# First pair of batches: one product M per batch, two pairs of heads side by side, in a new order of steps

## Chip, core, metric

The kernel runs on one core of one Trainium2 chip. The time is that of one execution in device microseconds; lower is better. In the texts PE or TensorE is the matmul engine (PEld its weight loads), DVE or VectorE, ACT or ScalarE, POOL or GpSimd the others, SP the engine that issues most DMAs. Times inside the execution count from the start of its span.

## The reference

Two attentions by way of 32 packed rows, then two feed-forward blocks; weights come as 64-bit floats and are converted on the chip.

```python
p_packed = sm_attn(p, k, v)              # 8 batches, 8 heads, 576 tokens, 64 dims, 32 packed rows
out = sm_attn(q, p_packed, p_packed)
x = out.transpose(0, 2, 1, 3).reshape(4608, 512)
a = x @ w1                               # 512 x 1024
b = x @ w2
x = ((a * b) @ w3) @ w_out               # 1024 x 1024, 1024 x 512
h = x @ w_in                             # 512 x 2048
return np.maximum(0.01 * h, h) @ w_out2  # 2048 x 512
```

## The kernel before

The eight batches are done as four pairs. For one batch, `a` and `b` are not made from the attention's output: the 32 packed rows of each head (ppM) are first multiplied with w1 and w2, which gives M, and the attention weights of the second softmax (AT, 4 heads x 32 rows = 128 partitions, in two units g of four heads) are then multiplied with M. Products that must be exact to nearly 32 bits are made of three passes over a number's high and low part (`three`); the parts come from a split: ScalarE casts the value to the high part, VectorE or GpSimd subtracts it.

The first pair (batches 0 and 1) has the weights' conversion beside it, and its order is written out by hand: `SCRIPT` is a list of steps, played one after the other. Each engine takes its instructions in a fixed order; a scheduler makes this order from the steps, and may move an instruction past some of another step. The steps that matter here, with unit u = 0, 1 for batch 0 and 2, 3 for batch 1:

- k, q, v, p: loads. s, e, n, t, y: scores, exponential, norm, transposition and values of the first attention, up to ppM. S, E, N, x: the same for the second, up to AT (x: ScalarE's cast and GpSimd's subtraction, L263 and L108).
- l, c, d with a key (w: w1 and w2 together, 16 pieces; o: w_out, 8; 3: w3, 16) and a number: load of a piece (L296, tile c64 with three buffers, 0.524 MB), conversion (ScalarE L278, VectorE L280 and L284), and GpSimd's addition (L287), for w with a store of the converted piece, which later pairs read back (L312).
- M, a, b: product M of a feature block fc (L406) and its splits for the first and the second batch (L425, L108). U packs the ppM of both batches in one tile pp32P of 128 columns. Z closes one set of PSUM pools and opens the next.
- A with fc, batch n, token half th: `ab_unit`, 12 matmuls of 288 columns for `a` and as many for `b` come as one step of 12 in the trace (L105, mm<-AT,M); ScalarE copies `a` (L460), VectorE multiplies (L462, here "product"), and the result is stored in DRAM. A step uses two of four PSUM tiles mm, so a step waits for the product of the step two before it.
- o, O, h, H: splits of w_out and of w3. W with fc and half: product of w3 and w_out (L105, mm<-ab,wsp), which makes the matrix W13; it needs mm tiles too.

Behind the script follow the x2 stage of the pair (mm<-ab,W), the other three pairs in loops, and the second feed-forward block.

Of the kernel before, what the change touches and what calls it, by code (L numbers as in the profile page):

```python
# [7 lines left out]

SCRIPT = """k2 k0 p0 s0 lw0 p1 k1 v0 cw0 lw1 k3 q0 e0 v2 s1 v1 s2 e1 n1 cw1 t0 lo0 n0 t1 lw2 dw0 e2 dw1 y0 S0 cw2 q1 v3 E0 s3 y1 n2 S1 q2 lw3 E1 lo1 t2 y2 lo2 e3 N0 co0 N1 x0 t3 S2 q3 x1 n3 E2 cw3 y3 U dw3 M0 N2 lw4 x2 co1 S3 dw2 Z cw4 lo3 dw4 a0 lw5 E3 lw6 N3 M1 x3 A000 b0 a1 A001 co3 do0 lw7 cw5 cw6 A011 do1 do3 A010 lo4 co2 dw5 do2 lw8 cw7 b1 A101 O1 dw6 A110 cw8 M2 lw11 dw8 co4 O0 A100 lw9 a2 dw7 cw9 lw10 A200 M3 A201 lo5 b2 O2 p2 a3 lw12 A210 dw9 A111 do4 cw10 p3 A211 lo6 A300 M4 b3 lw13 cw11 O3 A301 co5 A310 dw10 co6 o4 dw11 do5 a4 lo7 cw12 do6 b4 l30 A400 lw14 k4 lw15 A410 o5 o6 l31 A311 A411 dw12 M5 A401 co7 cw13 a5 l35 dw13 A501 do7 cw14 b5 c30 M6 cw15 A511 A510 o7 l33 a6 dw15 c31 b6 c35 d31 l37 A601 c33 dw14 d30 A600 l32 k6 M7 A611 H0 a7 k5 c37 b7 A610 c32 l34 A700 d33 d35 H3 d32 A701 d37 c34 h1 l38 d34 l315 H2 H5 H4 A711 h7 s4 c38 d38 W00 l36 c36 l39 l310 d36 h6 c39 l311 H8 e4 l312 W01 t4 A500 W10 W20 s5 c311 A710 v4 k7 d39 l313 d311 c310 c312 e5 c313 d310 h9 W30 v5 d312 H11 W21 h10 s6 l314 W11 n4 c314 d313 d314 q4 v7 W31 y4 t5 W40 s7 H12 q5 W41 h13 W50 n5 e6 v6 c315 d315 n6 H14 t6 W51 y5 e7 H15 y6 W60 n7 W61 W70 W71"""
KQ = {"k": 1}
F32 = mybir.dt.float32
F32R = mybir.dt.float32r
# [6 lines left out]
P = 128  # L21
# [11 lines left out]
def tile_kernel(ctx, tc, qT, kT, vL, pT, w12, w3b, wo1, win, wo2, out):  # L33
# [23 lines left out]
    def ps_m():  # L57
        return ps_pv() if psum["early"] else ps_tile([P, 512], "m", 2)
# [48 lines left out]
    def sub(engine, out, x, hi):  # L107
        engine.tensor_tensor(out=out, in0=x, in1=rd(hi), op=ALU.subtract)  # L108
# [79 lines left out]

    def att_t(b, g):
        pt = Ps.pop((b, g))  # L190
        if b < 2 and not psum["early"]:
            ps, tail = ps_m(), ps_m()
        else:
            t = ps_t()
            ps, tail = t[:, 0], t[:, 1]
        for c in range(4):
            nc.tensor.transpose(ps[:, c * P:(c + 1) * P], pt[:, c:512:4], ident)
        nc.tensor.transpose(tail[:64, :P], pt[:, 512:576], ident)
        PT = att.tile([P, 5, P], F32, tag="PT", name="PT", bufs=2)
        nc.scalar.copy(PT[:, 0:4].rearrange("p c s -> p (c s)"), ps)  # L200
        nc.scalar.copy(PT[:64, 4], tail[:64, :P])
        PTs[b, g] = PT

    def att_pv(b, g):


        PT = PTs.pop((b, g))
        _, st = s1p.pop((b, g))
        ps = ps_m() if b < 2 else ps_pv()
        v = [vs.pop((b, g, j)) for j in range(2)]  # L210
        for c in range(5):
            K = P if c < 4 else 64
            for j in range(2):
                r = slice(j * 64, j * 64 + 64)
                nc.tensor.matmul(ps[r, :P], PT[:K, c, r], v[j][:K, c, :], start=c == 0, stop=c == 4)  # L215
        pp = att.tile([P, P], F32, tag="pp", name="pp", bufs=1)
        nc.scalar.mul(pp, ps[:, :P], st[:, 3:4])
        nc.tensor.transpose(ps[:, 2 * P:3 * P], pp, ident)
        pv = ps[:, 2 * P:3 * P].rearrange("p (j c) -> p j c", j=2)
        for h in range(2):  # L220
            r = slice(h * 64, h * 64 + 64)
            nc.scalar.copy(ppM[b % 2][r, 2 * g:2 * g + 2, h * 32:h * 32 + 32], pv[r, :, h * 32:h * 32 + 32])

    def pair_up(p):

        for i in range(2):
            for j in range(2):
                c = (j ^ i) * 64
                x = ppM[i][:, j::2]
                if whole(2 * p):  # L230
                    nc.scalar.copy(pp32["P"][:, j::2, c:c + 64], x)
                else:
                    hi, lo = (ppP[:, a, j::2, c:c + 64] for a in range(2))
                    nc.scalar.copy(hi, x)
                    sub(nc.vector, lo, x, hi)

    def s2_mm(b, g):
        ps = scores(ppM[b % 2], "q", b, g, b % 2)
        t = att.tile([P, 18, 32], F32, tag="sT", name="sT", bufs=2)
        nc.vector.transpose(out=t.rearrange("p (a n) c -> p a (n c)", a=2), in_=ps[:, :, :TH])  # L240
        st = att.tile([P, 18, 2], F32, tag="st2", name="st2", bufs=2)
        nc.vector.tensor_reduce(out=st[:, :, 0:1], in_=t, axis=AX.X, op=ALU.max)
        nc.vector.tensor_tensor(out=t, in0=t, in1=st[:, :, 0:1].to_broadcast([P, 18, 32]), op=ALU.subtract)
        s2p[b, g] = t, st
# [318 lines left out]
    def attention_b(p):  # L563

        d = {s: [] for s in range(16)}
        for s, x in attention_a(p).items():
            if s >= 16:
                d[s - 16] += x
        us = units(p)
        for u, (b, g) in enumerate(us):  # L570
            s = (1, 4, 7, 10)[u]
            d[s] += [lambda b=b, g=g: s2_mm(b, g)]
            if u < 2:
                d[s + 1] += [lambda x=us[u + 2]: load_kq("q", *x)]
# [150 lines left out]
    def w13_step(fc, h):  # L725
# [11 lines left out]
        "d": lambda k, i: conv_end(k, i),  # L737
        "o": lambda i: split_wo1(i, nc.vector), "O": lambda i: split_wo1(i, nc.gpsimd),
        "h": lambda i: split_half("3", i, nc.gpsimd), "H": lambda i: split_half("3", i, nc.vector),
        "U": pack, "Z": late, "M": lambda i: m_mm(0, i), "a": lambda i: m_split(0, i, 0), "b": lambda i: m_split(0, i, 1),  # L740
        "A": ab_step, "W": w13_step,
        "r": lambda fc, th: reload_ab(0, fc, th), "f": lambda fc, th: split_ab(abr.pop((0, fc, th)), fc, th),
    }
    for x in SCRIPT.split():
        if x[0] in "lcd":
            steps[x[0]](x[1], int(x[2:]))
        elif x[0] in "AWrf":
            steps[x[0]](*(int(y) for y in x[1:]))
        else:
            steps[x[0]](*([int(x[1:])] if x[1:] else []))  # L750
# [293 lines left out]
```

## Time and profile before

| what | value |
|---|---|
| time, median of 3 runs | 1363.05 us (1358.98 to 1367.06) |
| the profiled execution: time / span | 1364.38 us / 1362.6 us |
| mean granted clock of TensorE | 0.988 |
| TensorE busy | 1315.1 us, 97% of the span |
| VectorE, ScalarE, GpSimd busy | 948.8, 701.1, 184.1 us |
| DMA | 323.48 MB, mean 237 GB/s |

The span runs from the first to the last instruction of the profiled execution; the 1.8 us between span and time lie around it. Busy times are sums over the engine's instructions; where instructions overlap a little or wait for a shared resource while they run, that is in them. The DMA share is the mean busy share of the core's 16 DMA engines.

### The profile page before, as it was taken

The numbers are of one execution on the slowest core, as the hardware profiler recorded it, in microseconds if no ns is written. First come the engines' busy times: TensorE is split into PE (matmuls) and PEld (weight loads), VectorE is DVE, ScalarE is ACT, GpSimd is POOL, SyncE is SP. The second block draws the span as 40 slices with busy tenths as digits, with TensorE's granted clock in tenths as the row PEclk, the third lists the DMA queues.
The fourth block names the chain that finished last, engine by engine and source line by source line (L and its number), as shares of the span: only waits on it lengthen the run. The fifth ranks groups of instructions, "written<-read, shape, count | busy, mean of one in ns | idle before, by whom it ended". The sixth has DMA issues, their size and how long they took to land.

```text
span 1362.6 us, 23490 instructions
## 1 busy us (share of the span) xinstructions
PE 1315.1 (97%) x8512; PEld 1255.7 (92%) x8512; DVE 948.8 (70%) x1588; ACT 701.1 (51%) x1365; POOL 184.1 (14%) x148
## 2 busy tenths in 40 slices
PE   6799999999999999999999999999999999999998
PEld 3578999989999999999999999999999999899997
DVE  4899668775987587762977665747665459486657
ACT  4566444675467556753755555545434434344332
POOL 1544521432133312200000000000000000000000
PEclk9799999999999999999999999999999999999999
DMA  9798658767985784397878976467545754878874
GB/s 306 250 304 283 224 158 253 234 200 223 302 280 185 256 271 139 98 307 246 307 262 280 328 260 227 166 209 252 177 152 208 250 187 151 285 260 307 292 265 151
DMA packets 174835, 323.48 MB, mean 237 GB/s; under 512 B 22656, under 2 KB 93312, under 8 KB 174720
## 3 DMA queue, kind: packets, MB, share of 16 engines
q1 hardware_dynamic: 153984, 300.74, 66.0%
q10 hardware_dynamic: 20736, 21.24, 4.5%
q8 instruction: 67, 1.10, 0.3%
q14 instruction: 48, 0.39, 0.1%
HBM read 226.75 MB, written 95.16 MB: 236 GB/s over the span
## 4 chain that ended last, share of the span: by engine, by line
PE 81%; DMA 8%; DVE 3%; issue 1%; ACT 1%; SPq 0%; ACTq 0%; DVEq 0%
PE mm L105 29%; PE b L899 26%; PE c L899 13%; PE a L899 7%; DMA xh<-xfd 4%; PE m L105 3%; PE at L163 2%; DMA c<-w3b 1%; PE at L215 1%; DVE cT L284 1%; DMA wi<-wid 1%; DVE cT L280 1%; DMA xl<-xfd 1%; DMA v<-vL 0%; DMA c<-w 0%
## 5 line engine op out<-in xcount | busy, mean ns | idle before, releaser
L105 PE MATMUL mm<-AT,M 128*128 128x288 f32 x1536 | 232.0, 302 | 13.9 <-DVE ab L462 4.1
L105 PEld LDWEIGHTS mm<-AT,M 128*128 128x128 f32 x1536 | 211.3, 190 | 27.4 <-ACT a L460 6.5
L899 PE MATMUL b<-xh,wi 128*128 128x384 f32 x768 | 218.7, 337 | 6.9 <-DMA xh<-xfd 5.6
L899 PE MATMUL b<-gh,wo 128*128 128x384 f32 x768 | 214.0, 336 | 1.4 <-DVE o L862 1.4
L105 PEld LDWEIGHTS mm<-ab,W 128*128 128x128 f32 x1536 | 204.4, 188 | 6.1 <-issue 5.5
L105 PE MATMUL mm<-ab,W 128*128 128x288 f32 x1536 | 209.9, 296 | 0.0
L899 PEld LDWEIGHTS b<-xh,wi 128*128 128x128 f32 x768 | 140.9, 188 | 9.6 <-DMA xh<-xfd 3.9
L899 PEld LDWEIGHTS b<-gh,wo 128*128 128x128 f32 x768 | 140.7, 188 | 2.0 <-issue 1.0
L899 PE MATMUL b<-xl,wi 128*128 128x384 f32 x384 | 128.9, 336 | 0.0
L899 PE MATMUL b<-gl,wo 128*128 128x384 f32 x384 | 128.6, 335 | 0.0
L667 ACT CAST gh<-gr 128x1152 fp32r<-128x1152 f32 (+1 forms) x72 | 75.6, 1052 | 68.9 <-PE b L899 32.2
L899 PE MATMUL c<-xh,wi 128*128 128x384 f32 x384 | 106.6, 337 | 2.9 <-DMA xh<-xfd 2.9
L899 PE MATMUL c<-gh,wo 128*128 128x384 f32 x384 | 107.3, 336 | 0.2
L108 DVE TENSOR_TENSOR gl<-gr,gh 128x1152 fp32r<-128x1152 f32 (+1 forms) x72 | 87.4, 1218 | 22.7 <-ACT gh L667 22.6
L287 POOL TENSOR_TENSOR c<-cT,c 128x512 int32<-128x512 int32 x56 | 77.7, 1390 | 166.7 <-DVE cT L284 68.7
L108 DVE TENSOR_TENSOR M<-m,M 64x512 fp32r<-64x512 f32 x124 | 84.3, 686 | 20.6 <-ACT M L425 18.1
L667 ACT CAST gh<-gs 128x1152 fp32r<-128x1152 f32 (+1 forms) x54 | 57.0, 1055 | 62.4 <-PE b L899 33.5
L108 DVE TENSOR_TENSOR ab<-ab,ab 128x288 fp32r<-128x288 f32 x128 | 66.5, 545 | 30.7 <-ACT ab L441 30.1
L108 POOL TENSOR_TENSOR wsp<-wsp 128x512 fp32r<-128x512 f32 x48 | 62.6, 1312 | 152.3 <-ACT wsp L385 121.2
L847 ACT ACTIVATE gr<-gr 128x1152 f32<-128x1152 f32 (+1 forms) x54 | 57.3, 1061 | 47.3 <-DVE gr L862 47.0
L425 ACT CAST M<-m 64x512 fp32r<-64x512 f32 x124 | 71.1, 580 | 17.3 <-PE m L105 5.5
L859 ACT COPY gr<-b 128x384 f32<-128x384 f32 x96 | 45.8, 478 | 56.5 <-PE b L899 55.0
(144 smaller groups left out, 2393.6 us busy)
## 6 DMA issues: line engine op xcount, KB each, us to landing
xh<-xfd SPq DMA_DIRECT2D x126, 384.0 KB, 5.4
xl<-xfd SPq DMA_DIRECT2D x126, 384.0 KB, 5.0
part<-o SPq DMA_DIRECT2D x48, 384.0 KB, 3.1
o<-part SPq DMA_DIRECT2D x48, 384.0 KB, 4.2
c<-wo SPq DMA_DIRECT2D x24, 512.0 KB, 5.0
wsp<-w12d SPq DMA_DIRECT2D x48, 256.0 KB, 3.1
abd<-ab ACTq DMA_DIRECT2D x80, 144.0 KB, 3.5
ab<-abd SPq DMA_DIRECT2D x80, 144.0 KB, 3.7
```

The costliest lines, as they stand in the source:

```text
L105: nc.tensor.matmul(dst, lhs(i), rhs(j), start=first and n == 0, stop=last and n == 2)
L108: engine.tensor_tensor(out=out, in0=x, in1=rd(hi), op=ALU.subtract)
L163: nc.tensor.matmul(ps[r:r + 64, th, :TH], w[:, 2 * g + j, :], x[:, th * TH:th * TH + TH], start=True, stop=True)
L215: nc.tensor.matmul(ps[r, :P], PT[:K, c, r], v[j][:K, c, :], start=c == 0, stop=c == 4)
L280: nc.vector.tensor_scalar(out=t, in0=hw, scalar1=3, scalar2=0x3FFFFFFF, op0=ALU.logical_shift_left, op1=ALU.bitwise_and)
L284: nc.vector.scalar_tensor_tensor(out=t, in0=hw, scalar=0xC0000000, in1=t, op0=ALU.bitwise_and, op1=ALU.bitwise_or)
L287: return lambda: nc.gpsimd.tensor_tensor(out=q, in0=t.bitcast(I32), in1=q, op=ALU.add)
L425: nc.scalar.copy(m[r, 0], ps[h ^ n][r])
L667: nc.scalar.copy(hi[step], x[step])
L847: nc.scalar.activation(out=out, in_=x, func=AF.Prelu, alpha=0.01)
L859: nc.scalar.copy(out, ps)
L899: nc.tensor.matmul(dst, lhs(l), rhs(r), start=first and n == 0, stop=last and n == total - 1, skip_group_check=True)
```

## The change

U and pp32P go: M is made for each batch from its own ppM. A matmul then has 64 columns of weights (two heads of 32 rows) instead of 128, and two of them, for j = 0 and 1, write the upper and the lower 64 partitions of one PSUM tile, so that the M of one batch stands in a tile of 128 partitions. Its split is then one cast and one subtraction of 128x512, where there were two and two of 64x512. The converted piece of w is held for two visits (`Wf`). Batch 1 of the first pair no longer has the heads of a pair swapped in its second scores. The other pairs keep their way, with both batches in one product.

```diff
-SCRIPT = """k2 k0 p0 s0 lw0 p1 k1 v0 cw0 lw1 k3 q0 e0 v2 s1 v1 s2 e1 n1 cw1 t0 lo0 n0 t1
...
+SCRIPT = """k0 p0 k1 lw0 v0 s0 v1 cw0 e0 q0 n0 s1 q1 t0 e1 lw1 n1 y0 t1 p1 k2 dw0 S0 y1 cw1
...
-        if b < 2 and not psum["early"]:
-            ps, tail = ps_m(), ps_m()
-        else:
-            t = ps_t()
-            ps, tail = t[:, 0], t[:, 1]
+        t = ps_t()
+        ps, tail = t[:, 0], t[:, 1]
...
-        ps = ps_m() if b < 2 else ps_pv()
+        ps = ps_pv()
...
-        ps = scores(ppM[b % 2], "q", b, g, b % 2)
+        ps = scores(ppM[b % 2], "q", b, g, 0 if alone(b) else b % 2)
...
-            if whole(2 * p):
-                w = converted("w", 2 * fc + g)
-                for j in range(2):
-                    nc.tensor.matmul(
-                        ps[j][:, g * 256:(g + 1) * 256], pp32["P"][:, 2 * g + j], w[:, j * 256:(j + 1) * 256],
-                        start=True, stop=True,
-                    )
-                continue
...
+    def m_alone(b, fc):
+        if fc not in Wf:
+            Wf[fc] = [converted("w", 2 * fc + g) for g in range(2)]
+        ps = ps_m()
+        for g, w in enumerate(Wf.pop(fc) if b else Wf[fc]):
+            for j in range(2):
+                tc.keep_in_program_order(
+                    nc.tensor.matmul(
+                        ps[j * 64:j * 64 + 64, g * 256:(g + 1) * 256], ppM[b][:, 2 * g + j],
+                        w[:, j * 256:(j + 1) * 256], start=True, stop=True,
+                    )
+                )
+        m_ps[b, fc] = ps
+
+    def split_alone(b, fc):
+        ps = m_ps.pop((b, fc))
+        m = main.tile([P, 2, 512], F32R, tag="M", name="M", bufs=3)
+        nc.scalar.copy(m[:, 0], ps)
+        sub(nc.vector, m[:, 1], ps, m[:, 0])
+        Mt[b, fc] = m
```

M and a now take a batch and a block (M03, a03), b is gone. The steps of batch 0 up to its first A steps come first, those of batch 1 behind them; the blocks' M run one A pair ahead; the loads of w_out and w3 come behind those of w; and the A steps A500 and A710, which stood between W steps, stand ahead of W00. From W00 on the script is otherwise as before. Where the order moves the instructions that the numbers below speak of:

TensorE around the first A step (mm<-AT,M). Before:

```order
L163 MATMUL at<-raw,ppM_76 64x288 x4
L218 MATMUL pv<-ident,pp 128x128
L406 MATMUL pv<-w_122,pp32P 128x256 x4
L163 MATMUL at<-raw,ppM_76 64x288 x4
L406 MATMUL m<-w_231,pp32P 128x256 x4
L105 MATMUL mm<-AT,M 128x288 x24
```

Now (ppM_75 is batch 0's, ppM_76 batch 1's; an A step is 12 matmuls):

```order
L425 MATMUL pv<-w_122,ppM_75 64x256 x4
L211 MATMUL pv<-v,PT 64x128 x10
L214 MATMUL pv<-ident,pp 128x128
L105 MATMUL mm<-AT,M 128x288 x12
L162 MATMUL at<-raw,ppM_76 64x288 x4
L105 MATMUL mm<-AT,M 128x288 x12
L425 MATMUL m<-w_294,ppM_75 64x256 x4
L162 MATMUL at<-raw,ppM_76 64x288 x4
L425 MATMUL m<-w_458,ppM_75 64x256 x4
L105 MATMUL mm<-AT,M 128x288 x48
L425 MATMUL m<-w_122,ppM_76 64x256 x4
L162 MATMUL at<-raw,ppad_73 64x288 x4
```

The second scores of batch 1 (at<-raw,ppM_76), which stood ahead of all A steps, now stand among those of batch 0; six A steps lie ahead of batch 1's first M (w_122 with ppM_76), and the seventh, A010, is the next mm<-AT,M behind the last row.

VectorE around the last transposition of batch 1's second softmax, from which its second AT is made. Before, with the first product (L462) behind it:

```order
L108 TENSOR_TENSOR M<-m,M 64x512
L280 TENSOR_SCALAR cT<-c_440 128x512
L255 TENSOR_TENSOR sT<-sT,st_426 128x576
L284 SCALAR_TENSOR_TENSOR cT<-c_440,cT 128x512
L257 STREAM_TRANSPOSE a_458<-sT 128x576
L462 TENSOR_TENSOR ab_485<-mm,a 128x288
```

Now:

```order
L170 TENSOR_REDUCE st<-at 128x1
L277 SCALAR_TENSOR_TENSOR cT<-c_666,cT 128x512
L248 TENSOR_TENSOR sT<-sT,st_499 128x576
L171 TENSOR_SCALAR st<-st 128x1
L273 TENSOR_SCALAR cT<-c_701 128x512
L250 STREAM_TRANSPOSE a_552<-sT 128x576
L277 SCALAR_TENSOR_TENSOR cT<-c_701,cT 128x512
```

Here a_552 stands behind six products and the conversion of the tenth piece of w (c_666) and with the eleventh (c_701), where a_458 stood ahead of the first product and behind the fifth piece of w.

VectorE at the last products ahead of W00. Before (ab_1422 is the 30th product; c_1337 is the seventh piece of w3):

```order
L462 TENSOR_TENSOR ab_1355<-mm,a 128x288
L280 TENSOR_SCALAR cT<-c_1337 128x512
L462 TENSOR_TENSOR ab_1380<-mm,a 128x288
L284 SCALAR_TENSOR_TENSOR cT<-c_1337,cT 128x512
L108 TENSOR_TENSOR ppP<-ppM_75,ppP 128x2x64 x2
L462 TENSOR_TENSOR ab_1422<-mm,a 128x288
```

Now (ab_1366 is the 31st product; c_1508 the eleventh piece of w3 in the order of SP's loads):

```order
L470 TENSOR_TENSOR ab_1314<-mm,a 128x288
L108 TENSOR_TENSOR M<-m,M 128x512
L108 TENSOR_TENSOR wsp<-c_1404,wsp 128x512
L273 TENSOR_SCALAR cT<-c_1508 128x512
L277 SCALAR_TENSOR_TENSOR cT<-c_1508,cT 128x512
L470 TENSOR_TENSOR ab_1366<-mm,a 128x288
L470 TENSOR_TENSOR ab_1396<-mm,a 128x288
```

All 32 products now stand ahead of W00's results, and more conversions of w3 ahead of the last of them.

## Rows read from the trace of the kernel before

**Rows 1.** Busy us of each engine, clock, DMA share and GB/s by stretch

```profile
0.00:37.00 37.00, 24.49 (x159) 14.00 (x159) 16.50 (x35) 14.09 (x35) 8.39 (x15) 0.89 0.90 297
37.00:60.00 23.00, 14.41 (x65) 9.53 (x63) 22.10 (x35) 13.48 (x28) 11.61 (x10) 0.80 0.69 245
60.00:135.00 75.00, 68.61 (x461) 61.37 (x461) 68.68 (x126) 50.02 (x111) 35.32 (x29) 0.96 0.92 295
135.00:160.00 25.00, 23.29 (x186) 22.10 (x187) 18.02 (x30) 11.92 (x25) 15.20 (x11) 0.97 0.64 205
160.00:189.40 29.40, 29.40 (x244) 29.40 (x244) 13.93 (x25) 10.83 (x26) 9.80 (x7) 0.97 0.44 135
```

**Rows 2.** Timeline of TensorE: start us, us, instructions, idle time before

```profile
135.01 1.92 PE L105 MATMUL mm<-ab,wsp 128*128 128x256 f32 x14 [1.61 <-DVE ab L462]
...
141.57 1.74 PE L105 MATMUL mm<-AT,M 128*128 128x288 f32 x12
...
189.39 3.08 PE L105 MATMUL mm<-ab,W 128*128 128x288 f32 x22
```

**Rows 3.** SP's waits to 135 us: total, times, longest

```profile
SPq L296 <- DVE cT L284: 43.5, 20, 8.2
```

**Rows 4.** Groups of VectorE, 60 to 138 us: count, busy us, mean ns

```profile
L284 DVE SCALAR_TENSOR_TENSOR cT<-c,cT 128x512 uint32<-128x512 uint32 x23 | 20.9, 917 | 0.1
L108 DVE TENSOR_TENSOR M<-m,M 64x512 fp32r<-64x512 f32 x26 | 17.8, 685 | 0.7 <-ACT M L425 0.2
L280 DVE TENSOR_SCALAR cT<-c 128x512 uint32<-128x512 uint32 x23 | 14.0, 628 | 3.4 <-POOL ab L108 1.8 <-DMA c<-w 0.8 <-DMA c<-w3b 0.5
L462 DVE TENSOR_TENSOR ab<-mm,a 128x288 f32<-128x288 f32 x30 | 13.3, 449 | 1.6 <-PE mm L105 0.8 <-ACT a L460 0.4
L108 DVE TENSOR_TENSOR wsp<-c,wsp 128x512 fp32r<-128x512 f32 x3 | 3.9, 1288 | 0.0
```

**Rows 5.** Groups of ScalarE, 0 to 190 us

```profile
L425 ACT CAST M<-m 64x512 fp32r<-64x512 f32 x28 | 16.1, 580 | 4.3 <-PE m L406 1.5 <-DVE M L108 1.4 <-PE mm L105 1.0
...
L200 ACT COPY PT<-t 128x512 f32<-128x512 f32 x4 | 2.3, 582 | 2.4 <-PE t L198 2.4
```

**Rows 6.** Timeline of TensorE's matmuls, 102.99 to 111.06 us

```profile
102.99 1.02 PE L406 MATMUL m<-w,pp32P 128*128 128x256 f32 x4
103.67 1.15 PE L105 MATMUL mm<-AT,M 128*128 128x288 f32 x6
104.75 1.19 PE L163 MATMUL at<-raw,ppad 128*64 128x288 f32 x8
105.87 5.32 PE L105 MATMUL mm<-AT,M 128*128 128x288 f32 x38
111.06 1.10 PE L406 MATMUL m<-w,pp32P 128*128 128x256 f32 x4
```

**Rows 7.** Groups of VectorE, 0 to 60 us, second softmax: longest, shortest operation

```profile
L255 DVE TENSOR_TENSOR sT<-sT,st 128x576 f32<-128x576 f32 x4 | 3.7, 925 | 0.1
...
L254 DVE RECIPROCAL st<-st 128x18 f32<-128x18 f32 x4 | 1.0, 244 | 0.0
```

**Rows 8.** Timeline of VectorE: first product, and 30th ahead of W00

```profile
60.10 0.82 DVE L462 TENSOR_TENSOR ab<-mm,a 128x288 f32<-128x288 f32 x2
...
137.47 0.44 DVE L462 TENSOR_TENSOR ab<-mm,a 128x288 f32<-128x288 f32 x1
```

**Rows 9.** DMA from 0 to 135 us: packets, bytes, mean rate

```profile
DMA packets 21910, 38.75 MB, mean 287 GB/s; under 512 B 5454, under 2 KB 9998, under 8 KB 21899
```

**Rows 10.** Two shorter stretches, columns as in rows 1

```profile
50.00:60.00 10.00, 5.74 (x38) 4.55 (x38) 9.90 (x16) 5.96 (x11) 5.29 (x4) 0.97 0.29 97
...
80.00:135.00 55.00, 50.75 (x359) 45.16 (x357) 50.69 (x97) 37.90 (x85) 22.38 (x18) 1.00 0.93 302
```

**Rows 11.** Group of GpSimd, 0 to 138 us: subtraction of AT's split

```profile
L108 POOL TENSOR_TENSOR AT<-a,AT 128x576 fp32r<-128x576 f32 x4 | 6.9, 1735 | 6.0 <-ACT AT L263 5.8
```

**Rows 12.** Timeline of weight loads of the scores in rows 6

```profile
104.74 0.68 PEld L163 LDWEIGHTS at<-raw,ppad 128*64 128x64 f32 x8 [0.16 <-issue]
```

More of the change, by code (lines that the diff above doesn't have):

```diff
@@ L7 @@
 from concourse.masks import make_identity
-SCRIPT = """k2 k0 p0 s0 lw0 p1 k1 v0 cw0 lw1 k3 q0 e0 v2 s1 v1 s2 e1 n1 cw1 t0 lo0 n0 t1 lw2 dw0 e2 dw1 y0 S0 cw2 q1 v3 E0 s3 y1 n2 S1 q2 lw3 E1 lo1 t2 y2 lo2 e3 N0 co0 N1 x0 t3 S2 q3 x1 n3 E2 cw3 y3 U dw3 M0 N2 lw4 x2 co1 S3 dw2 Z cw4 lo3 dw4 a0 lw5 E3 lw6 N3 M1 x3 A000 b0 a1 A001 co3 do0 lw7 cw5 cw6 A011 do1 do3 A010 lo4 co2 dw5 do2 lw8 cw7 b1 A101 O1 dw6 A110 cw8 M2 lw11 dw8 co4 O0 A100 lw9 a2 dw7 cw9 lw10 A200 M3 A201 lo5 b2 O2 p2 a3 lw12 A210 dw9 A111 do4 cw10 p3 A211 lo6 A300 M4 b3 lw13 cw11 O3 A301 co5 A310 dw10 co6 o4 dw11 do5 a4 lo7 cw12 do6 b4 l30 A400 lw14 k4 lw15 A410 o5 o6 l31 A311 A411 dw12 M5 A401 co7 cw13 a5 l35 dw13 A501 do7 cw14 b5 c30 M6 cw15 A511 A510 o7 l33 a6 dw15 c31 b6 c35 d31 l37 A601 c33 dw14 d30 A600 l32 k6 M7 A611 H0 a7 k5 c37 b7 A610 c32 l34 A700 d33 d35 H3 d32 A701 d37 c34 h1 l38 d34 l315 H2 H5 H4 A711 h7 s4 c38 d38 W00 l36 c36 l39 l310 d36 h6 c39 l311 H8 e4 l312 W01 t4 A500 W10 W20 s5 c311 A710 v4 k7 d39 l313 d311 c310 c312 e5 c313 d310 h9 W30 v5 d312 H11 W21 h10 s6 l314 W11 n4 c314 d313 d314 q4 v7 W31 y4 t5 W40 s7 H12 q5 W41 h13 W50 n5 e6 v6 c315 d315 n6 H14 t6 W51 y5 e7 H15 y6 W60 n7 W61 W70 W71"""
+SCRIPT = """k0 p0 k1 lw0 v0 s0 v1 cw0 e0 q0 n0 s1 q1 t0 e1 lw1 n1 y0 t1 p1 k2 dw0 S0 y1 cw1 k3 lw2 E0 S1 s2 v2 dw1 N0 E1 e2 v3 lw3 x0 N1 n2 s3 cw2 t2 x1 e3 dw2 n3 y2 M00 t3 lw4 q2 a00 y3 cw3 Z A000 S2 dw3 A001 lw5 M01 a01 E2 A100 cw4 q3 N2 A101 S3 dw4 lw6 cw5 x2 dw5 M02 a02 E3 A200 cw6 N3 lw7 A201 dw6 cw7 x3 lw8 M10 a10 dw7 A010 A011 M03 a03 cw8 A300 lw9 A301 dw8 cw9 M11 a11 lw10 dw9 A110 A111 M04 a04 cw10 A400 lw11 A401 dw10 cw11 M12 a12 lw12 dw11 A210 lo0 A211 M05 a05 cw12 A500 lw13 A501 dw12 co0 cw13 M13 a13 lw14 dw13 do0 A310 A311 lo1 M06 a06 cw14 A600 O0 lw15 A601 co1 dw14 cw15 lo2 do1 M14 a14 dw15 co2 O1 A410 lo3 do2 A411 M07 a07 co3 lo4 O2 A700 do3 co4 lo5 A701 M15 a15 O3 do4 l30 A510 co5 lo6 do5 o4 A511 c30 co6 l31 M16 a16 o5 p2 A610 d30 lo7 do6 c31 A611 o6 l33 M17 a17 co7 d31 H0 l35 do7 c33 A710 h1 p3 o7 A711 k4 d33 c35 l32 H3 d35 l37 c32 H5 d32 l34 c37 H2 k5 d37 c34 l38 k6 l315 d34 H4 h7 s4 c38 d38 W00 l36 c36 l39 l310 d36 h6 c39 l311 H8 e4 l312 W01 t4 W10 W20 s5 c311 v4 k7 d39 l313 d311 c310 c312 e5 c313 d310 h9 W30 v5 d312 H11 W21 h10 s6 l314 W11 n4 c314 d313 d314 q4 v7 W31 y4 t5 W40 s7 H12 q5 W41 h13 W50 n5 e6 v6 c315 d315 n6 H14 t6 W51 y5 e7 H15 y6 W60 n7 W61 W70 W71"""
@@ L148, in load_p, with alone @@
             nc.sync.dma_start(out=ppad[b % 2][r, :, h * 32:h * 32 + 32], in_=pT[r, b])
-    pp32 = {}
-    def whole(b):
+    def alone(b):
         return b < 2
@@ L222, in att_pv, with pair_up @@
             nc.scalar.copy(ppM[b % 2][r, 2 * g:2 * g + 2, h * 32:h * 32 + 32], pv[r, :, h * 32:h * 32 + 32])
-    def pair_up(p):
+    def pair_up():
         for i in range(2):
@@ L229, in pair_up @@
                 x = ppM[i][:, j::2]
-                if whole(2 * p):
[L231 to L235, printed above, removed]
+                hi, lo = (ppP[:, a, j::2, c:c + 64] for a in range(2))
+                nc.scalar.copy(hi, x)
+                sub(nc.vector, lo, x, hi)
     def s2_mm(b, g):
-        ps = scores(ppM[b % 2], "q", b, g, b % 2)
+        ps = scores(ppM[b % 2], "q", b, g, 0 if alone(b) else b % 2)
         t = att.tile([P, 18, 32], F32, tag="sT", name="sT", bufs=2)
@@ L402, in m_mm @@
         for g in range(2):
-            if whole(2 * p):
-                w = converted("w", 2 * fc + g)
-                for j in range(2):
-                    nc.tensor.matmul(
-                        ps[j][:, g * 256:(g + 1) * 256], pp32["P"][:, 2 * g + j], w[:, j * 256:(j + 1) * 256],
-                        start=True, stop=True,
-                    )
-                continue
             w = Ws.pop(("w", 2 * fc + g)).rearrange("p a (b c) -> p a b c", b=2)
@@ L429, in m_split @@
         Mt[2 * p + n, fc] = m
+    Wf = {}
+    def m_alone(b, fc):
[17 more added lines that the diff above has]
+        Mt[b, fc] = m
     def m_unit(p, fc):
@@ L577, in attention_b @@
             d[s + 3] += [lambda b=b, g=g: s2_split(b, g)]
-        d[5] += [lambda: pair_up(p)]
+        d[5] += [lambda: pair_up()]
         d[8] += [lambda: load_w(0), lambda: load_w(1)]
@@ L709, in tile_kernel @@
     us = units(0) + units(1)
-    def pack():
-        pp32["P"] = att.tile([P, 5, P], F32, tag="PT", name="pp32P", bufs=2)[:, 0:4]
-        pair_up(0)
     def late():
@@ L739, in tile_kernel @@
         "h": lambda i: split_half("3", i, nc.gpsimd), "H": lambda i: split_half("3", i, nc.vector),
-        "U": pack, "Z": late, "M": lambda i: m_mm(0, i), "a": lambda i: m_split(0, i, 0), "b": lambda i: m_split(0, i, 1),
+        "Z": late, "M": m_alone, "a": split_alone,
         "A": ab_step, "W": w13_step,
@@ L746, in tile_kernel @@
             steps[x[0]](x[1], int(x[2:]))
-        elif x[0] in "AWrf":
+        elif x[0] in "AWMarf":
             steps[x[0]](*(int(y) for y in x[1:]))
```

## The prediction

> **What bounds the kernel now.** I read the busy table of long stretches first, for the change touches only the part ahead of the x2 stage of the first pair. [...] Then the timeline of TensorE: W00 begins at 135.01 us, the first x2 unit at 189.39 us [rows 2]. Behind 189.39 nothing is changed, so the change is worth what it moves this one time; and from W00 on TensorE hardly waits. So the question is when W00 can start.
>
> Who sets that? From 60 to 135 us VectorE is busy 68.68 of 75 us, TensorE 68.61, and the DMA share is 0.92 [rows 1]. Three resources stand at 92% at once. What SP waits for says the same: its loads of weight pieces waited 43.5 us for VectorE's conversions, that is for one of the three buffers c64 [rows 3]. A relief of VectorE alone is worth only as much as the loads and TensorE let through.
>
> **The change, part by part.** *Splits of M.* Before, each feature block needs four casts and four subtractions on 64 partitions (32 + 32 for the pair); now two and two on 128. A 64x512 subtraction took 685 ns [rows 4], a 64x512 cast 580 ns [rows 5]. The trace has no 128x512 split of M; the nearest row is the copy PT<-t out of PSUM, 128x512 in 582 ns [rows 5], so time goes with the 512 elements, not with the partitions. At that price 16 + 16 go: 11.0 us of VectorE and 9.3 us of ScalarE. If the wide ones cost double, nothing is saved; I take the row. The four copies that packed pp32P go too; ScalarE is not near its limit (50 of 75 us, [rows 1]).
>
> *The products for M.* Half a block, four records, took 0.68 us to the next start (102.99 to 103.67), so 1.36 us a block for both batches. Now there are two visits with 64 columns of weights, two pairs of heads side by side. That shape is in the trace: the scores, eight records of 128x64 with 288 columns, took 1.12 us between two A steps (104.75 to 105.87) [rows 6]; for 256 columns 1.0 us. Eight blocks go from 10.9 to 16 us: 5 us more for TensorE, one of the three at 92%.
>
> *The start.* S0 now stands behind batch 0 alone. In SP's order 3.54 MB lie up to the load of q0; at the 297 GB/s of the first 37 us [rows 1] they are there at about 13 us. With copies, values and scores behind them I put VectorE's first transposition of S0 at 16.5 us. From there to its first product (order of VectorE) stand four first and five second operations of a conversion (0.628 and 0.917 us, [rows 4]), two units of the second softmax of eight operations from 0.925 to 0.244 us, 5.4 us a unit [rows 7], and small rows: 20.9 us. With about 1 us of waiting for ScalarE's exponential, the first product comes at 38.5 us, against 60.1 [rows 8].
>
> *VectorE from there.* Up to the product that W00 waits for (the 31st) I count in the order 28 conversions at 0.628 + 0.917 us = 43.3, 31 products at 0.449 = 13.9, 15 splits of M at 0.685 = 10.3, three of w3 at 1.288 = 3.9 [rows 4], the second batch's two units 10.7 [rows 7], and 8.4 of small rows: 90.5 us. 38.5 + 90.5 = **129 us**. The same count for before gives 78.4 us for 30 products, and they took 77.8 (60.10 to 137.91, [rows 8]), so the prices hold. That was with 23 conversions: the new order has five more in this stretch. So 21 us of earlier start and 11 us of saved work come out as little.
>
> *The loads.* The conversion of piece c_1508 now stands ahead of the 31st product. SP's order has 35.55 MB up to it, and 30 stores of A results of 0.147 MB make 40.0 MB. Before, 38.75 MB were moved by 135 us [rows 9]; the shares of [rows 1] sum to 118 us, so 328 GB/s while the engines are busy. That is 122 us if they never rest, and 40.0/0.302 = **132 us** at the 302 GB/s that the trace holds from 80 to 135 us [rows 10]. The hole of the old start (0.29 from 50 to 60 us, [rows 10]), while VectorE did four units of softmax, should go.
>
> *TensorE.* Here is what the new order adds: A010, the first step of batch 1, stands in TensorE's queue ahead of M03 and all that follows, and needs the second unit's AT. Its last transposition (a_552) is 23.2 us of VectorE behind the first product, by the same prices: 38.5 + 23.2 = 61.7 us. A cast of 0.7 and GpSimd's subtraction of 1.735 us [rows 11] follow: **64 us**. Only six A steps, M00 to M02, M10 and some attention, about 20 us, lie ahead of it from 37 us on, so TensorE waits there for some microseconds. Behind it stand 26 A steps at 1.64 us (12 records; 38 from 105.87 to 111.06, [rows 6]), twelve M at 1.0 and 8 us of attention: 62.6 us, or 68.5 us at the 0.915 of TensorE from 60 to 135 us. 64 + 68.5 = **132.5 us**.
>
> The three ends are 129, 132 and 132.5 us. Where three queues of fixed order meet, the last sets the time, and a little is lost between them: I take **W00 at 133 us**. *Behind W00:* from 135.01 to 189.39 are 54.4 us, of which A500 and A710 (24 records, 3.3 us; A500 begins at 141.57, [rows 2]) are now done ahead: 51.1, and 50.3 with half of the 1.7 us of waiting left out. The x2 stage starts at 183.3 instead of 189.4 us: **6.1 us earlier**. The profiled run has 1364.4 us with a span of 1362.6, so 1358.3 by its own time; the median of the three runs shown, 1363.05, is 1.3 below it: 1357 us.
>
> **Rivals.** *(a) The loads set the pace throughout.* If they run no better than the old mean of 287 GB/s [rows 9], 40.0 MB need 139 us, W00 follows at 140.5, x2 at 190.8: 1364.5 us, no change. For it: three buffers still, and SP waiting on VectorE. Against it: the hole at 50 to 60 us is in that mean.
>
> *(b) More is gained.* If the conversions wait less for GpSimd (0.917 us for an operation over 512 elements, where a subtraction over as many takes 0.685, [rows 4]), 28 of them save 6.5 us; and TensorE waits 3% instead of 8.5%: W00 at 127 to 128, x2 at 178: 1351.5 us.
>
> *(c) Slower, by the wait of A010.* TensorE takes its queue in order, so each microsecond that the second AT is late moves M03 and all later steps by one. At 64 us it costs nothing beyond the sum; from 77 us on the kernel is slower by more than 0.5% (6.1 + 6.8 us later). An AT at 80 us gives W00 at 149, x2 at 199: 1373 us. For it: GpSimd has the conversions' additions and the AT subtractions in one queue, each behind a load. Against it: 13 us is the time of seven loads of 0.524 MB.
>
> [...]
>
> **Chances.** A measurement of this kernel can tell about 0.5% (6.8 us) from no change. The forecast, W00 at 130 to 136, has 0.45; its 3 to 9 us straddle that bound: 0.18 faster, 0.27 same. (a) 0.18 and (d) 0.02, same. (b) 0.22, faster. (c) 0.13, slower. So faster 0.40, same 0.47, slower 0.13. The range goes from below (b), with 2 us for what VectorE may save besides, 1349.5, to past (a), 1366.5; most of (c) and a little of (b) are left out. The forecast's own range is 1354 to 1360.
>
> **What would show it.** Right: the first product near 38.5 us; TensorE idle for several microseconds ahead of the seventh A step, which begins near 64 us; sixteen casts and sixteen subtractions 128x512 for M at 0.58 and 0.69 us; W00 near 133 us; a DMA share over 0.9 from 40 to 125 us. Wrong: 128x512 splits near 1.2 us; M visits of more than 1.1 us; a seventh A step past 75 us (c); VectorE idle on weight pieces for more than 10 us between 70 and 130 us (a); or idle time of TensorE in the W steps, which the old order had filled with A500 and A710.

## The result and the profile after

The changed kernel takes 1378.95 us (median of 7 runs, 1375.27 to 1380.09); the kernel before took 1365.38 us beside it (7 runs, 1358.98 to 1369.42). The ratio is 1.010, 95% interval 1.0076 to 1.0123: slower by 10 to 17 us. Run again, both gave a ratio of 1.0065 (1.0041 to 1.009). The forecast was 1357.0 us, with a range from 1349.5 to 1366.5; the time lies past its end.

Busy time by stretch in the changed kernel, columns as in [rows 1]; the last row ends where the x2 stage begins:

```profile
0.00:37.00 37.00, 23.71 (x164) 14.57 (x164) 21.54 (x44) 16.93 (x40) 10.90 (x17) 0.91 0.94 316
37.00:60.00 23.00, 18.26 (x121) 14.39 (x122) 18.46 (x34) 8.01 (x16) 6.67 (x6) 0.93 0.98 330
...
60.00:135.00 75.00, 57.65 (x373) 45.71 (x374) 55.72 (x91) 36.93 (x82) 35.67 (x29) 0.90 0.71 234
135.00:160.00 25.00, 24.93 (x180) 21.58 (x180) 18.72 (x33) 11.19 (x25) 9.04 (x7) 0.90 0.83 255
160.00:199.20 39.20, 39.20 (x342) 38.73 (x340) 18.67 (x33) 17.91 (x44) 16.27 (x12) 1.00 0.41 126
```

The start is won: taken together, TensorE is busier up to 60 us than in [rows 1] (42.0 us in place of 38.9), and so are the loads (a DMA share of 0.94 and 0.98, in place of 0.90 and 0.69). Then, from 60 to 135 us, none of the three resources that stood at 92% is near its limit: TensorE 57.65 of 75 us, VectorE 55.72, DMA share 0.71. With room in all three, a serial chain is the suspect. TensorE's timeline shows the marks of the forecast (A010's two halves, W00, first x2 unit):

```profile
63.89 0.80 PE L105 MATMUL mm<-AT,M 128*128 128x288 f32 x4 [0.96 <-ACT AT L256]
65.38 2.29 PE L105 MATMUL mm<-AT,M 128*128 128x288 f32 x8 [0.69 <-POOL AT L108]
...
151.43 0.74 PE L105 MATMUL mm<-ab,wsp 128*128 128x256 f32 x4
...
199.20 3.08 PE L105 MATMUL mm<-ab,W 128*128 128x288 f32 x22
```

A010 comes at 63.89 us, as forecast (64). W00 comes at 151.43 instead of 133 us, x2 at 199.20 instead of 183.3 (before: 189.39, [rows 2]). So the loss lies between A010 and W00. TensorE's waits up to 155 us (total, times, longest) name it:

```profile
PE mm L105 <- ACT M L435: 11.0, 8, 2.5
...
PE mm L105 <- DVE M L108: 5.2, 5, 2.8
```

The A steps wait 16.2 us for the split of M. In the kernel before, the only such row up to 135 us is

```profile
PE mm L105 <- DVE M L108: 1.6, 2, 0.9
```

In the timeline of TensorE after the change the reader can see where:

```profile
92.17 1.08 PE L425 MATMUL m<-w,ppM 128*64 128x256 f32 x8
94.95 1.92 PE L105 MATMUL mm<-AT,M 128*128 128x288 f32 x8 [1.70 <-ACT M L435]
97.18 3.12 PE L105 MATMUL mm<-AT,M 128*128 128x288 f32 x16 [0.32 <-DVE M L108]
100.23 1.08 PE L425 MATMUL m<-w,ppM 128*64 128x256 f32 x8
102.00 3.45 PE L105 MATMUL mm<-AT,M 128*128 128x288 f32 x24 [0.69 <-ACT M L435]
105.38 1.08 PE L425 MATMUL m<-w,ppM 128*64 128x256 f32 x8
108.23 1.32 PE L105 MATMUL mm<-AT,M 128*128 128x288 f32 x8 [1.77 <-ACT M L435]
110.51 2.39 PE L105 MATMUL mm<-AT,M 128*128 128x288 f32 x16 [0.96 <-DVE M L108]
```

In the script each M visit stands directly ahead of the A pair that reads it. Where both waits show, the pair's first 8 records wait for the cast and the other 16 for the subtraction, and in these rows nothing else is in TensorE's queue between. The section on the change says that "the blocks' M run one A pair ahead". That is wrong: the script has `M03 a03 cw8 A300`, the product, its split and its own A pair, one behind the other. Before, M3 stood ahead of A201, and its first reader, A300, came four A steps later.

Where attention stands between the two, the pair can start at once:

```profile
74.83 1.08 PE L425 MATMUL m<-w,ppM 128*64 128x256 f32 x8
75.75 1.14 PE L162 MATMUL at<-raw,ppad 128*64 128x288 f32 x8
76.82 3.44 PE L105 MATMUL mm<-AT,M 128*128 128x288 f32 x24
```

Of the twelve pairs behind A010, five start so and seven wait (two of these with a shorter piece of attention between), 13.9 us in all.

Not all of a wait is the split itself. Ahead of 102.00 us the wait is 0.69 us for the cast, and the subtraction (on VectorE from 101.98 to 102.67 us) is done beside the pair's first records: this is the split alone. The longer waits have a queue in them. In ScalarE's order a cast can stand behind the store of an A result or a conversion. Timeline of ScalarE (ACTq is its sequencer, which issues the store):

```profile
87.30 0.81 ACTq L100 DMA_DIRECT2D abd<-ab  x2
88.16 0.59 ACT L435 CAST M<-m 128x512 fp32r<-128x512 f32 x1 [2.31 <-DMA abd<-ab]
88.64 1.22 ACT L271 ACTIVATE w<-c 128x512 int32<-128x512 uint32 x2
```

The cast ran at 88.16 us behind two stores of the previous pair. On VectorE it is the subtraction that stands behind other work. The longest wait, from the timelines of ScalarE, VectorE and TensorE:

```profile
128.58 0.60 ACT L435 CAST M<-m 128x512 fp32r<-128x512 f32 x1
...
131.06 1.43 DVE L108 TENSOR_TENSOR ab<-c,ab 128x256 fp32r<-128x256 f32 x1
132.41 1.51 DVE L273 TENSOR_SCALAR cT<-c 128x512 uint32<-128x512 uint32 x1
133.84 0.68 DVE L108 TENSOR_TENSOR M<-m,M 128x512 fp32r<-128x512 f32 x1
...
134.57 4.21 PE L105 MATMUL mm<-AT,M 128*128 128x288 f32 x16 [2.84 <-DVE M L108]
```

The cast is done at 129.2 us; the subtraction begins 4.7 us later, behind two splits of w_out, a product and conversions.

There is a second suspect. From 62.19 to 71.52 us SP issues nothing, since a load of the second pair's k (raw<-kT, L124) waits for a buffer that a score on TensorE frees, and weight pieces stand behind it. Its waits on that, up to 150 us:

```profile
SPq L124 <- PE at L162: 14.1, 4, 9.0
```

### The profile page after: what moved, and what is told of

Read it like the earlier page. It is cut to its first block, busy times and chain, and to the rows that moved or that the text cites. A ratio compares the mean times of both kernels' runs of the same rounds, so it can differ in the third digit from the quotient of the medians.

```text
span 1377.2 us, 23581 instructions
## 1 busy us (share of the span) xinstructions
PE 1320.8 (96%) x8576; PEld 1255.9 (91%) x8576; DVE 942.6 (68%) x1572; ACT 691.1 (50%) x1345; POOL 182.2 (13%) x148
## 4 chain that ended last, share of the span: by engine, by line
PE 80%; DMA 10%; DVE 5%; issue 1%; SPq 1%; ACT 1%; POOL 1%; ACTq 0%; DVEq 0%; POOLq 0%
PE mm L105 30%; PE b L903 25%; PE c L903 13%; PE a L903 6%; DMA xh<-xfd 4%; PE m L105 2%; PE at L162 2%; DMA xl<-xfd 2%; PE at L211 1%; DMA c<-w 1%; DMA part<-o 1%; DMA wsp<-w12d 1%; DVE cT L273 1%; DMA c<-w3b 1%; DVE ab L108 1%
## 5 line engine op out<-in xcount | busy, mean ns | idle before, releaser
L105 PEld LDWEIGHTS mm<-AT,M 128*128 128x128 f32 x1536 | 214.2, 193 | 41.0 <-ACT M L435 15.2
L903 PE MATMUL b<-xl,wi 128*128 128x384 f32 x384 | 130.1, 339 | 0.3
L108 DVE TENSOR_TENSOR gl<-gr,gh 128x1152 fp32r<-128x1152 f32 (+1 forms) x72 | 87.5, 1220 | 21.3 <-ACT gh L675 21.3
L108 DVE TENSOR_TENSOR M<-m,M 64x512 fp32r<-64x512 f32 (+1 forms) x111 | 75.3, 686 | 22.3 <-ACT M L410 15.6
L108 DVE TENSOR_TENSOR ab<-ab,ab 128x288 fp32r<-128x288 f32 x128 | 65.0, 533 | 32.6 <-ACT ab L449 31.9
L108 POOL TENSOR_TENSOR wsp<-wsp 128x512 fp32r<-128x512 f32 x48 | 62.6, 1313 | 153.8 <-ACT wsp L378 118.8
L470 DVE TENSOR_TENSOR ab<-mm,a 128x288 f32<-128x288 f32 x128 | 57.3, 452 | 33.6 <-ACT a L468 17.0
```

Source lines behind the costliest of these rows:

```text
L105: nc.tensor.matmul(dst, lhs(i), rhs(j), start=first and n == 0, stop=last and n == 2)
L470: nc.vector.tensor_tensor(out=t, in0=pb[:, :TH], in1=a, op=ALU.mult)
L903: nc.tensor.matmul(dst, lhs(l), rhs(r), start=first and n == 0, stop=last and n == total - 1, skip_group_check=True)
```

## Experiments

Theory 1: the serial chain M, cast, subtraction, A, exposed wherever nothing else stands between M and A. Theory 2: SP's queue is held by the k loads. Rival 3: the narrow M visits cost the time. Rival 4: the A steps' place among conversions and loads.

**The A pairs one place later.**

```diff
-... M10 a10 dw7 A010 A011 M03 a03 cw8 A300 lw9 A301 dw8 cw9 M11 a11 lw10 dw9 A110 A111 ...
+... M10 a10 dw7 A200 A201 M03 a03 cw8 A010 lw9 A011 dw8 cw9 M11 a11 lw10 dw9 A300 A301 ...
```

> Every A pair from A200 on is moved back by one place in the script, so that a block's M and its split stand one A pair ahead of the steps that read them; all else keeps its order. Theory 1 (exposed chain: M, cast, subtraction, A, one behind the other, since each M stands directly ahead of its own A pair): TensorE's waits of the A steps for the cast and the subtraction of M, 11.0 + 5.2 us up to 150 us in the changed kernel, fall under 5 us, W00 starts 10 us earlier, near 141 us, the x2 stage near 189, time near 1368 us. Theory 2 (SP stands behind the second pair's k loads, the weight pieces come late): the hole in the loads from 62 to 75 us stays, W00 stays within 3 us of 151, time 1376 to 1379. Rival 3 (the narrow M visits themselves cost the time): nothing changes, 1379.

Measured: 1362.43 us, ratio 0.9971 (0.9944 to 0.9997). W00 at 134.1 us, x2 at 185.22, further than theory 1 asked. The waits for M fall to 1.6 us. TensorE's timeline:

```profile
92.96 1.08 PE L425 MATMUL m<-w,ppM 128*64 128x256 f32 x8
94.39 3.44 PE L105 MATMUL mm<-AT,M 128*128 128x288 f32 x24 [0.35 <-ACT a L468]
97.76 1.08 PE L425 MATMUL m<-w,ppM 128*64 128x256 f32 x8
98.78 3.44 PE L105 MATMUL mm<-AT,M 128*128 128x288 f32 x24
```

Behind the M at 97.76 the A pair starts without a wait, for it reads the M before. That speaks against theory 2 (the k loads stand in SP's order as in the changed kernel) and against rival 3 (the visits are the same).

**The second pair's k loads held back.**

```diff
+            ld = nc.sync.dma_start(out=t, in_=(kT if key == "k" else qT)[b, 2 * g + j])
+            if key == "k" and b in (2, 3):
+                tc.keep_in_program_order(ld)
```

> The k loads of the second pair are kept at their place in the script, so that from the third of these eight on they stand in SP's queue behind the loads of the weights and no longer at 57 to 72 us. Theory 2 (SP's queue): SP issues weight pieces through 62 to 72 us, the hole goes, and W00 starts up to 9 us earlier, 142 to 145 us; time 1369 to 1373. Theory 1 (exposed chain): the pieces come earlier but every A pair still waits for its own M, so W00 moves by less than 3 us; time 1376 to 1379.

Measured: 1381.43 us, ratio 1.0116 (1.0084 to 1.0147); W00 at 150.8, x2 at 204.3. The hole gets deeper, not filled: from 62 to 75 us 98 GB/s where the changed kernel had 142. What SP waits for now, up to 155 us:

```profile
SPq L291 <- DVE cT L279: 44.0, 20, 4.0
SPq L291 <- ACT w L273: 23.5, 7, 11.4
```

The k loads are out of SP's way, and now the weight pieces wait for a buffer c64 that the conversions keep: their first operation (ACT w) stands in ScalarE's queue among casts of M and copies that wait for TensorE. So with the k loads out of the way the hole stays and W00 does not move: theory 2 falls. The x2 stage is later still because attention of the second pair now lies behind W00 (466 TensorE records in the W phase, 410 in the changed kernel).

**The new form of M in the old order** (each `M3` written as `M03 M13`, `a3` as `a03`, `b3` as `a13`, U dropped).

> The order of before with the new form of M alone: for each block the M of batch 0 and of batch 1 in two visits with 64 columns of weights, one 128x512 cast and subtraction each; packing gone. If the form is what costs (rival 3): eight blocks at two visits of 1.0 us instead of one of 1.36 us and more, slower than before by 3 us or more, above 1367 us. Theories 1 and 2 (the order is what costs): W00 within 3 us of 135, time 1358 to 1365 us, no slower than before.

Measured: 1368.24 us, ratio 1.0014 (0.9992 to 1.0036); W00 at 130.1, x2 at 189.33. The median is over 1367, but the interval holds no change and the x2 stage is where it was: the form costs nothing that can be measured, and brings nothing. (W00 is 4.9 us earlier than before, but 458 TensorE records lie between it and the x2 stage, where before had 428; so W00 alone is not the measure.) Rival 3 has no support.

**M not pinned.**

```diff
-                tc.keep_in_program_order(
-                    nc.tensor.matmul(
...
-                )
+                nc.tensor.matmul(
...
```

> The changed kernel without the pin that keeps M's matmuls behind all TensorE work written ahead of them; the scheduler may now move them, and spreads quarter visits among the A steps, about half an A pair ahead. Theory 1: the A steps' waits for M's split fall from 16 us to about 8, W00 near 145, time near 1372. If the pin were no part of the chain, or theory 2 alone holds: W00 within 3 us of 151, time 1376 to 1379.

Measured: 1364.04 us, ratio 0.9979 (0.9962 to 0.9996); W00 at 136.1, x2 at 187.00, better than expected. The A steps (count; busy us, mean ns of one, which overlap; idle before them up to 155 us, by cause) hardly wait for M:

```profile
L105 PE MATMUL mm<-AT,M 128*128 128x288 f32 x384 | 61.7, 309 | 1.6 <-DVE st L171 1.1 <-ACT M L433 0.5
```

Without the pin the scheduler parts the visits and puts quarter visits up to an A pair ahead. The change has no chain without the pin: `keep_in_program_order` held each M behind all A steps written ahead of it.

**No data chain, own order.** From A300 on each pair reads the M made one place earlier, that of the other batch; every instruction stays, but the result is another one.

```diff
+        if b < 2 and made.index((b, fc)) > 3:
+            m = Mt[made[made.index((b, fc)) - 1]]
```

> The changed kernel in its own order, but from the A steps of A300 on each pair reads the M that was made one place earlier in the order, which is the other batch's, so the result is another one; all instructions are still there, and each M visit still stands directly ahead of an A pair. Theory 1 (what costs is that an A pair waits for the cast and subtraction of the M made just ahead of it): the waits for M fall below 5 us, W00 starts near 135 to 138 us, time 1364 to 1368. Rival 4 (it is the place of the A steps among conversions and loads, which the run with the A pairs one place later changed as well): W00 stays above 147 us, 1375 or more.

Measured: 1364.76 us, ratio 0.9991 (0.9974 to 1.0007); W00 at 133.02, x2 at 184.36 us. The M visits still stand ahead of A pairs, and the pairs start behind them without a wait:

```profile
83.42 1.08 PE L425 MATMUL m<-w,ppM 128*64 128x256 f32 x8
84.43 3.44 PE L105 MATMUL mm<-AT,M 128*128 128x288 f32 x24
```

The waits for M fall from 16.2 to 1.6 us. With the two runs that take the waits away by other means (the A pairs later, M not pinned), theory 1 is shown. Rival 4 is not parted from it quite cleanly: the script is unchanged, but the scheduler makes the engines' orders anew, and at W00 VectorE has done 30 conversions, where the changed kernel has done 34. From A010 to W00 (columns as in [rows 1]), first the changed kernel:

```profile
63.89:151.43 87.54, 71.95 (x469) 57.47 (x469) 65.91 (x108) 43.55 (x97) 41.41 (x34) 0.88 0.72 229
```

and without the chain:

```profile
62.96:133.02 70.06, 65.45 (x452) 51.91 (x452) 54.18 (x95) 39.03 (x91) 36.01 (x29) 0.98 0.73 246
```

The 17.5 us between them are 11.0 us less idle time (15.6 against 4.6) and 6.5 us less busy time. In the busy part are 17 records more (some 2.5 us, an estimate at 65.45 us for 452) and the clock, 0.88 against 0.98. In the second, the loads have the same hole (146 GB/s from 62 to 75 us), and W00 still comes at 133: the loads were not the bound.

**Both remedies.** 

> The A pairs one place later and M's matmuls not pinned, both. If both are remedies for the same chain, the second adds nothing: W00 at 132 to 136, time 1361 to 1364, within 0.3% of either alone. If the pin cost something of its own: x2 stage near 183, time 1360 or less.

Measured: 1363.83 us, ratio 0.9986 (0.9966 to 1.0006), W00 at 137.5, x2 at 188.40. The second remedy adds nothing; a cost of the pin of its own does not show.

**A pairs later, `H0 H3 H2` as `h0 h3 h2`** (splits of w3 by GpSimd). 

> The A pairs one place later, and three of the five splits of w3 ahead of W00 done by GpSimd in place of VectorE (3 x 1.29 us). If VectorE sets the end once the chain is gone (busy 34.97 of 35 us from 100 to 135 us with the A pairs one place later): W00 3 to 4 us earlier, 130 to 131 us, time near 1359. If GpSimd, with 21 of these 35 us, holds the conversions back instead, or the loads set the end: W00 within 1.5 us of 134, or later; time 1362 or more.

Measured: 1363.91 us, ratio 0.999 (0.997 to 1.001). W00 came at 139.24 us, but the profiled execution, 1370.87 us, was the longest of its ten. No gain; whether VectorE or GpSimd held it, this run does not tell.

**Old order, M late.** The lines show the old order with the new form of M, then this run.

```diff
-... A200 M03 M13 A201 lo5 a12 O2 p2 a03 lw12 A210 dw9 A111 do4 cw10 p3 A211 lo6 A300 ... a13 ...
+... A200 A201 lo5 O2 p2 lw12 A210 dw9 A111 do4 cw10 p3 A211 lo6 M03 M13 a03 a13 A300 ...
```

> The reverse: the old order with the new form of M, in which both M of a block and their splits, from block 1 on, stand directly ahead of the block's first A step, where before they stood further ahead. Theory 1: seven exposed chains in place of none; about 1 us of wait each, for the second M visit lies beside the first split: the A steps wait 5 to 10 us for M, W00 5 to 8 us later than the 130.1 us of the old order with the new form, time 1372 to 1376. If the place of M doesn't matter: W00 within 2 us of 130, time 1368.

Measured: 1367.56 us, ratio 1.0008 (0.9987 to 1.003). The waits for M are there, up to 155 us:

```profile
PE mm L105 <- ACT M L435: 3.4, 4, 1.6
...
PE mm L105 <- DVE M L108: 1.7, 4, 0.9
```

W00 moves from 130.1 to 134.5 us, somewhat less than the 5 to 8 us asked for. But the x2 stage starts at 190.04 against 189.33 us, and the time doesn't move: my expectation of 1372 to 1376 was a miss. The W phase gave it back (55.6 us in place of 59.2). Its waits were not for the splits of w3: in both runs they are for the split of W13 (DVE W L108), 2.5 us in place of 3.5. The larger part is busy time, and goes with the clock: 457 records in 53.0 us at a granted clock of 1.00, in place of 458 in 55.7 us at 0.94. So the reverse brings the waits back, and the loss in time is not shown by it.

**Both kernels again, and two of the others again.**

> The changed kernel once more, to see how far the part behind the start of the x2 stage varies between executions of one program: in its first profile that part took 1178.0 us, 4.8 us more than the 1173.2 of before, though nothing is changed there. If that is variation: W00 near 151 and the x2 stage near 199 again (within 2 us), but the part behind it anywhere from 1172 to 1180 us. If the change slows the later stages: 1177 to 1179 us again, and the kernel before, run again, near 1173. Ratio to before 1.008 to 1.012 in either case.

> The kernel before once more, as the other half of that comparison and as a measure of what no change looks like: ratio 1.000 with an interval that holds it, x2 stage near 189.4 us. If the later stages vary by themselves, the part behind the x2 start differs by 2 us or more from 1173.2; if not, it is within 1 us of it.

> The A pairs one place later once more, on one chip with the next run, for a closer ratio. If the 4.2 us by which the x2 stage began earlier than before are really won: ratio 0.995 to 0.998 with an interval below 1, x2 stage at 183 to 187 us. If the first ratio of 0.9971 was luck: 0.999 or more.

> The changed kernel without the data chain once more (another result, as there). By the sum of the prediction, x2 stage 6.1 us ahead of before, ratio 0.9955; the first run showed the stage at 184.4 us, 5.0 us ahead, but a ratio of 0.9991. If the earlier start is won: 0.995 to 0.998, as with the A pairs one place later. If something behind the x2 stage gives it back: 0.999 or more again.

The x2 start of the changed kernel, then of the kernel before, in these executions:

```profile
200.46 1.75 PE L105 MATMUL mm<-ab,W 128*128 128x288 f32 x12
```

```profile
186.36 3.08 PE L105 MATMUL mm<-ab,W 128*128 128x288 f32 x22
```

| kernel | x2 start, us | span behind it, us | ratio to before, 95% |
|---|---|---|---|
| before | 189.39 | 1173.2 | |
| before, again | 186.36 | 1171.6 | 1.000 (0.9976 to 1.0023) |
| changed | 199.20 | 1178.0 | 1.010 (1.0076 to 1.0123) |
| changed, again | 200.46 | 1172.9 | 1.0065 (1.0041 to 1.009) |
| A pairs later | 185.22 | 1176.7 | 0.9971 (0.9944 to 0.9997) |
| A pairs later, again | 188.36 | 1170.6 | 0.999 (0.9972 to 1.0008) |
| no data chain | 184.36 | 1178.6 | 0.9991 (0.9974 to 1.0007) |
| no data chain, again | 186.06 | 1179.3 | 1.0002 (0.9982 to 1.0023) |

In the second execution of the changed kernel W00 comes at 152.68 us, and the waits for M are 8.2 and 5.5 us; the ratio, 1.0065, lies under the 1.008 to 1.012 that I expected. The kernel before, again, has its x2 start 3 us off the 189.4 expected, and 1171.6 us behind it, between the two marks set (within 1 us of 1173.2, or 2 us off).

The span behind x2 is the span less the x2 start. In one and the same program it differs by up to 6 us, and the x2 start by up to 3 us. So the 4.8 us that the changed kernel first seemed to lose behind the x2 stage are variation: in its second execution the part took 1172.9. With the A pairs later the kernel is at the level of before or a few tenths of a per cent under it; the two intervals, 0.9944 to 0.9997 and 0.9972 to 1.0008, don't settle more, and by the expectation set for the second run, 0.999 or more means that the first ratio was luck. It beats the changed kernel plainly: 1362.4 against 1376 to 1379 us.

## Why the prediction was wrong

**Right.** The first product came at 38.69 us (38.5), A010 at 63.89 (64). That they fit to tenths is luck: in the second execution they came at 43.30 and 65.86. The 128x512 splits cost what the 64x512 had cost; groups of the changed kernel up to 155 us:

```profile
L108 DVE TENSOR_TENSOR M<-m,M 128x512 fp32r<-128x512 f32 x15 | 10.2, 681 | 4.6 <-ACT M L435 4.5
L435 ACT CAST M<-m 128x512 fp32r<-128x512 f32 x15 | 8.8, 584 | 12.6 <-PE m L425 8.5 <-DMA abd<-ab 2.3 <-DVE cT L273 1.6
```

An M visit took 1.0 us (97.76 to 98.78 with the A pairs later), and its weight loads lay beside it: in the changed kernel's visit at 105.38 us, 0.63 us of PEld beside 1.08 us of PE,

```profile
105.38 0.63 PEld L425 LDWEIGHTS m<-w,ppM 128*64 128x64 f32 x8 [0.17 <-issue]
```

so rival (d), of chance 0.02, falls: it had these loads add their own time to the visits, at the 0.68 us of [rows 12] 8.2 us for the twelve behind A010, and a visit would have taken 1.7 us. Rival (a) falls too: the DMA share over 0.9 that was forecast did not come, but loads at 234 GB/s from 60 to 135 us were not what W00 waited for; without the chain they ran at 246 GB/s from A010 on, and W00 came at 133.02. Rival (b) did not come either: even without the chain W00 was not at 127 to 128 us (and 64 + 62.6/0.97, TensorE's part of that rival, is 128.5).

**Wrong: the share of 0.915 for TensorE behind A010.** The prediction has "62.6 us, or 68.5 us at the 0.915 of TensorE from 60 to 135 us. 64 + 68.5 = 132.5". The steps took 87.5 us, a share of 0.715. The 0.915 belongs to an order in which M ran ahead of its use; it was carried into one where it doesn't, so the wait of each A pair for the M made just ahead of it stood at nothing in the sum. It measured 13.9 us behind A010, and the clock fell besides (0.88, without the chain 0.98). With the chain taken out these steps took 70.06 us, a share of 0.893, and W00 came at 133.02: the rest of TensorE's sum holds. The ends for VectorE (129) and the loads (132) are not tested by that run, since fewer conversions lie ahead of its W00.

The rows to price it stood in the document: a cast of 580 ns [rows 5] and a subtraction of 685 ns [rows 4] between an M and its pair, 1.27 us for each of the twelve M behind A010, 15.2 us if all of it is exposed, and the clock besides. W00 at 132.5 + 15.2 = 147.7, x2 at 198: slower by 9 us, where 10 to 17 were measured. That 15.2 comes near the 13.9 us of waits is luck, though: the split alone exposes 0.69 us, in the seven pairs that wait 4.8 us, and the other 9 us are casts and subtractions that stood behind other work on ScalarE and VectorE, which these rows do not price.

**Rival (c)** had the right sign and 1373 us, but its mechanism did not happen: A010 was on time. The list of rivals lacked the chain. The ends of 129 and 132 us could not show it either, since they count work and no waits.

**Behind W00** the phase took 47.8 us in place of 50.3 (in that sum the 1.7 us of waiting are the 25.00 us from 135 to 160 less TensorE's 23.29, [rows 1]): it has 410 records, and 428 without the chain, where it took 51.3 us with 1.3 us of waiting; what is missing of the second pair's attention lies ahead of W00 there (469 records from A010 on, 452 without the chain). So 3.6 of the 18.4 us between the two were given back by the x2 start.

**The gain of 6.1 us** was reckoned from one execution's 189.39. In the second, the x2 stage of before starts at 186.36. Without the chain the stage starts at 184.4 and 186.1 us, some 3 us ahead of the mean of before, and no gain shows in the ratios. What stays open is whether those 3 us are won or given back behind the x2 stage: that part was longer in both executions without the chain (1178.6 and 1179.3 us, before 1173.2 and 1171.6), but the variation of one program there is as large.

## What to carry to other kernels

A matmul whose operand passes through other engines first needs other work between its producer and itself in TensorE's queue (here the waits for M were 16.2 us, and 1.6 with the A pairs one place later): look in the order at what stands between each product and its reader, and price an empty gap at the cast (0.69 us here) and at what stands ahead of the cast and of the subtraction in their engines' queues (up to 4.7 us here). A busy share belongs to an order, not to an engine (TensorE's from 60 to 135 us: 0.915 before, 0.77 in the changed kernel); carry it to a new order only after its chains have been compared. And a pin that fixes an order also takes from the scheduler the means to mend it: one place in the script, or the pin alone, was worth all that the change lost.

## What the runs showed of the hardware

With the waits for M goes a lower clock: in the changed kernel the granted clock is 0.88 from A010 to W00, without the data chain 0.98. A part of both is a slow group behind A010 that has nothing to do with M: 8 records took 2.29 us (at 65.38 us in the changed kernel, at 64.45 without the chain), behind waits of 0.96 and 0.69 us for AT; from 63.89 to 71.40 us the changed kernel's clock is 0.55. From the first A pair behind that on, the clock is 0.91 in the changed kernel (71.42 to 151.43 us) and 1.00 without the chain (69.10 to 133.00 us). It falls behind the two longest waits for M: 24 records took 4.75 us at 116.39 us, behind a wait of 2.48 us (clock 0.72 from 116 to 122 us), where 24 took 3.44 us at 88.80, behind 1.64 us; 16 records took 4.21 us at 134.57 us, behind 2.84 us (clock 0.60 from 134 to 141.2 us), where 16 took 2.39 us at 110.51, behind 0.96 us. It does not go by the length of the wait alone: behind 1.70 us (at 94.95) 8 records took 1.92 us at a clock of 0.62, behind 1.77 us (at 108.23) 1.32 us at 1.00.

A cast and a subtraction of 128x512 out of PSUM cost what those of 64x512 cost: 584 and 681 ns against 580 and 685 ns.
